# Batch 1's key maxima spread by ScalarE, and ordered behind a product of batch 0

## The chip, the cores and the metric

The kernel runs on one core of a Trainium2 chip. The metric is device time in microseconds, the median of some runs. Engines are called PE (TensorE, matmuls), DVE (VectorE), ACT (ScalarE), POOL (GpSimd) and SP (SyncE, here the queue that issues the DMAs). Each works through its own list of instructions in order; they meet through semaphores.

## What is computed

Attention over local keys and block summaries, then two feed-forward blocks. Cut to what matters here:

```python
B, H, S, D = 2, 8, 768, 64
k_sum = k.reshape(B, H, nb, 32, D).max(axis=3)       # nb = 24 blocks of 32 keys: the key maxima
v_sum = v.reshape(B, H, nb, 32, D).mean(axis=3)
scores_l = scale * q @ k.T                            # only |i - j| < 16 counts
scores_s = scale * q @ k_sum.T + log(32)              # every query sees every block
a = softmax(concat([masked scores_l, scores_s]))
x = a @ concat([v, v_sum])
x = sigmoid(xr @ w_r) * (relu(xk @ w_k) ** 2 @ w_v)   # xk, xr: mixes of x with x one row earlier
u = x + (relu(x.T @ w_tok1) @ w_tok2).T
out = u + relu(u @ w_ch1) @ w_ch2
```

## The kernel before

Attention works on six query tiles of 128 rows for each of the two batches. For a tile t the keys that its queries may see, and the 24 block maxima, stand in one tile kw: the local keys in the middle, and a copy of the maxima at either end, so that one matmul gives 120 scores. `k_max` (line 231) reduces the keys of a tile to 4 maxima with DVE, into ks. `kw_sums` (line 237) copies all 24 maxima of ks to both ends of a kw: two copies a tile, twelve a batch, and none can start before the last of the six reductions. `s_stage` multiplies queries by kw (sp, line 309), DVE reads the scores with the mask and takes the row minimum (pe and mn, line 327), ACT takes the exponential (line 329). For batch 1 `n_stage` then normalises on POOL (line 340) with a reciprocal from DVE (line 338), `t_stage` transposes (pt, line 346) and `v_stage` multiplies by the values (pv, line 366). For batch 0 the normalisation comes after that: the sums' reciprocals are spread by a matmul (rb, line 382), ACT copies pv into xT (line 385) and DVE multiplies (line 386). That is the product of x.

While attention runs, PE is filled with the first feed-forward block of the rows that are ready: `mixed` makes xk (POOL line 466, DVE line 467), its rounded upper part xh (ACT) and the rest xl (DVE, line 469); ko is xk times w_k (line 477); `k2_tile` takes relu (rl, ACT line 489), the square (DVE line 490), and splits it in kh (ACT line 491) and kl (POOL line 492); acc is that times w_v. There is one bank for ko, so the next ko waits until ACT has read the last one. The weights are 64-bit numbers that are rounded piece by piece in `Weights.step`: ACT (wst, line 148), DVE (wf, lines 152 and 158), ACT (w, line 160), POOL (its low half, line 161); there are two wf buffers, so a piece's first DVE step waits for POOL's step of the piece two before.

The program is written by hand as a mix of generators, and then a scheduler reorders each engine's list by its own estimate of durations and by priorities (`tc.high_priority`, the numbers HK, HM and so on). `behind(inst, marks)` (line 171) adds a rule for that scheduler that an instruction stands after another one. So a change at one place moves instructions at others. Batch 1 begins in `prep(1)`, which is reached while batch 0's last two tiles are still in work: key loads have come by then, and the six reductions, two value sums and the copies of the maxima are written there.

Of the kernel before, what the change touches and what calls it, by code (L numbers as in the profile page):

```python
# [14 lines left out]
ALU = mybir.AluOpType  # L15
AX = mybir.AxisListType
# [38 lines left out]
def fused_kernel(ctx, tc, q, k, v, vt, mu, w_k, w_v, w_r, w_t1, w_t2, w_c1, w_c2, out):  # L55
    nc = tc.nc
# [7 lines left out]
    NB = S // BLOCK  # L64
# [13 lines left out]
    def bank(tag, bufs, shape, name):  # L78
        return ps.tile(shape, F32, tag=tag, bufs=bufs, name=name)
# [88 lines left out]
    def in_line(inst):  # L168

        behind(inst, line[-1:])  # L170
        line.append(inst)

    def behind(inst, marks):

        for m in marks:
            tc.add_manual_dep(inst.ins, m.ins.name,
                              mybir.DependencyInfo(mybir.DependencyClass.NoSync, mybir.DependencyReason.DATA), reason="queue order")
# [23 lines left out]
    def ahead(n):  # L201

        def wrap(fn):
            def run(*args, **kw):
                with tc.high_priority(n) if n else ExitStack():
                    return fn(*args, **kw)
            return run
        return wrap
# [17 lines left out]
    def k_max(b, t):  # L226

        st = state[b]
        keys = st["kw"][t][:, :, K0 + PAD:K0 + PAD + 128].rearrange("p a (n w) -> p a n w", w=BLOCK)
        n = 128 // BLOCK  # L230
        nc.vector.tensor_reduce(st["ks"][:, :, n * t:n * t + n], keys, AX.X, ALU.max)

    @ahead(HK)
    def kw_sums(b, t):
        st = state[b]
        for o in (0, WC - NB):
            nc.gpsimd.tensor_scalar(st["kw"][t][:, :, o:o + NB], st["ks"], 1.0, 1.0, ALU.mult, ALU.mult)

    @ahead(HL)
    def vt_load(b, j):  # L240
# [112 lines left out]
    @ahead(HV)  # L353
    def v_stage(zs):
        b, t, _ = zs[0]["u"]
        st = state[b]
        if t not in st["pv"]:
            st["pv"][t] = bank("pv", 1, [128, NP, 128], "pv")
        pv = st["pv"][t]
        line.clear()  # L360
        for p in range(NP):
            for half in range(2):
                for z in zs[::-1]:
                    e = z["u"][2]
                    h = 2 * p + e
                    m = nc.tensor.matmul(pv[64 * e:64 * e + 64, p, 64 * half:64 * half + 64],  # L366
                                         st["vw"][t][half][0][:, h * D:(h + 1) * D],
                                         z["PT"][:, p, 64 * half:64 * half + 64], start=True, stop=True)
                    if len(zs) > 1:
                        in_line(m)  # L370
        if zs[-1]["u"][2] == 1:
            c0 = b * XB + 1 + 128 * t
            if b not in LATE:
                nc.scalar.copy(xT[:, :, c0:c0 + 128], pv)
            else:
                den = st["den"].pop(t)
                nc.vector.tensor_scalar(den, den, 1e-9, None, ALU.add)
                nc.vector.reciprocal(den, den)
                rb = bank("pt", 2, [128, NP, 128], "rb")
                for p in range(NP):  # L380
                    for e in range(2):
                        nc.tensor.matmul(rb[64 * e:64 * e + 64, p], den[:, e, p:p + 1].to_broadcast([128, D]), ident,
                                         start=True, stop=True)
                x = xT[:, :, c0:c0 + 128]
                nc.scalar.copy(x, pv)
                nc.vector.tensor_tensor(x, x, rb, ALU.mult)

    done_tiles = [0]

    def attention():  # L390
        slots = {}
# [2 lines left out]
        for i in range(len(steps) + 1):  # L394
            if i < len(steps):
                b, t, es = steps[i]
                if b and t == 0:
                    yield from prep(b)
                zs = s_stage(b, t, es)
                if len(es) == 1:  # L400
                    for what, z, lag in zip((t_stage, v_stage), (zs[0], zs), LAGS):
                        slots.setdefault(min(i + lag, n0), []).append(((i + lag, lag), what, z))
                else:
                    slots[i + 1] = [((i, 1), n_stage, z) for z in zs] + [((i, 2), t_stage, z) for z in zs] + [((i, 3), v_stage, zs)]
                if i < SPIN_UNITS:
                    spin(SPIN)
                yield 0.95 * len(es)
                if es[-1] == 1 and t + 1 < NT:
                    kw_sums(b, t + 1)
                if t == 0 and es[-1] == 1 - b * (len(es) == 1):  # L410
                    if b == 0:
                        v_gather(b)
                    vw_sums(b, 0)
# [34 lines left out]
    def prep(b):  # L448

        for t in range(NT):  # L450
            k_max(b, t)
            yield HOLD / (NT + 2)
        for j in range(2):
            vt_sum(b, j)
            yield HOLD / (NT + 2)
        kw_sums(b, 0)
        v_gather(b)
# [121 lines left out]
    for kind in range(3):  # L579
        mc = const.tile([128, NC], F32, name=f"mask{kind}")  # L580
        mm = work.tile([128, 2, 128], F32, tag="t32", bufs=2, name="mm")
        for half in range(2):
            m = mm[:, half, :NC]
            nc.gpsimd.memset(m, 0.0)
            first = 64 * half - PAD
            keys = m[:, NB:NC] if half == 0 else m[:, 0:NK]
# [10 lines left out]
    for t in range(NT):  # L597
        ahead(HK)(k_max)(0, t)
    kw_sums(0, 0)
    for j in range(2):  # L600
        vt_sum(0, j)
# [264 lines left out]
```

## Time and profile before

| what | value |
|---|---|
| median of 3 runs | 511.06 us (510.78 to 512.84) |
| the profiled execution | 511.19 us, span 509.4 us |
| PE busy | 492.6 us (97% of the span) |
| DVE, ACT, POOL busy | 249.1, 206.4, 186.4 us |
| granted clock of PE, mean | 0.998 |

The span runs from the first to the last instruction; the execution's own time is 1.8 us longer. Times in the views count from the start of the span. Batch 1's attention begins near 66 us and ends near 180 us; after about 255 us the second feed-forward block keeps PE busy to the end. In a timeline, a row merges neighbours of one kind, and a matmul of sp, pv or rb is recorded twice (x18 for nine).

### The profile page before, as it was taken

The page shows a single profiled execution, that of the slowest core. Times are in us where ns is not written, and L with a number is a line of the kernel's source. Part 1 is how long each engine was busy: PE and PEld are TensorE (multiplying, and loading weights), DVE is VectorE, ACT ScalarE, POOL GpSimd, SP SyncE. Part 2 cuts the span into 40 slices and gives each one's busy share as a digit, 9 for nine tenths or more (in the row PEclk, how much of TensorE's full clock was granted, in tenths as well). Part 3 has the DMA queues.
Part 4 walks back from the last instruction along what each step waited for, and adds up shares of the span by engine and source line. Part 5 has one row for each costly group of instructions (what it writes and reads, how often), then busy time and mean ns, then how long its engine had stood idle before and what let it go on. Part 6 is the DMA issues. An engine that isn't in the chain of part 4 may idle for free.

```text
span 509.4 us, 7950 instructions
## 1 busy us (share of the span) xinstructions
PE 492.6 (97%) x3064; PEld 399.6 (78%) x3064; DVE 249.1 (49%) x544; ACT 206.4 (41%) x477; POOL 186.4 (37%) x250
## 2 busy tenths in 40 slices
PE   7999897999999999999999999999999999999995
PEld 3578775788888888887888888888888888888884
DVE  3789999740515174798676576343141211311112
ACT  1689655962534444556455435343110201001000
POOL 5335567971534465697734333332100000000000
PEclk9999999999999999999999999999999999999999
DMA  8999942031000660001525650000020000200002
GB/s 254 307 295 338 333 128 71 9 100 40 21 0 14 237 248 0 1 0 42 164 85 209 235 176 1 0 1 1 0 84 0 1 0 1 82 1 0 0 1 82
DMA packets 24197, 45.40 MB, mean 89 GB/s; under 512 B 2112, under 2 KB 11328, under 8 KB 24160
## 3 DMA queue, kind: packets, MB, share of 16 engines
q1 hardware_dynamic: 24160, 44.90, 28.1%
q8 instruction: 24, 0.39, 0.3%
q14 instruction: 13, 0.11, 0.1%
HBM read 41.16 MB, written 3.15 MB: 87 GB/s over the span
## 4 chain that ended last, share of the span: by engine, by line
PE 79%; DVE 9%; POOL 4%; issue 3%; ACT 2%; DMA 2%; SPq 1%; DVEq 0%; POOLq 0%; ACTq 0%
PE o L791 19%; PE go L477 19%; PE ko L477 10%; PE acc L477 10%; PE ro L477 5%; PE ho L477 3%; PE h L477 3%; PE sp L309 3%; PE pv L366 2%; DVE xk L467 2%; PE pt L346 2%; DMA xT<-in_vt_dram 1%; PE spin L556 1%; DVE wf L152 1%; PE utr L745 1%
## 5 line engine op out<-in xcount | busy, mean ns | idle before, releaser
L477 PE MATMUL go<-u,w 128*128 128x512 f32 x432 | 106.7, 393 | 0.0
L161 POOL TENSOR_TENSOR w<-wf,w 128x512 fp32r<-128x512 f32 x50 | 68.7, 1379 | 85.5 <-ACT w L160 78.8
L477 PEld LDWEIGHTS go<-u,w 128*128 128x128 f32 x432 | 80.7, 188 | 17.5
L791 PE MATMUL o<-w,gh 128*128 128x512 f32 x288 | 89.0, 395 | 0.0
L706 DVE SCALAR_TENSOR_TENSOR gl<-go,gh 128x512 fp32r<-128x512 f32 x36 | 24.9, 691 | 121.1 <-ACT gh L705 120.9
L477 PE MATMUL ko<-xh,w 128*128 128x256 f32 x384 | 77.0, 289 | 0.7 <-ACT w L160 0.6
L705 ACT ACTIVATE gh<-go 128x512 fp32r<-128x512 f32 x36 | 21.5, 597 | 128.8 <-PE go L477 128.7
L477 PEld LDWEIGHTS ko<-xh,w 128*128 128x128 f32 x384 | 61.4, 188 | 4.5 <-issue 1.3
L791 PEld LDWEIGHTS o<-w,gh 128*128 128x128 f32 x288 | 54.0, 188 | 12.1
L477 PE MATMUL acc<-w,kh 128*128 128x512 f32 x192 | 60.7, 398 | 1.9 <-ACT kh L491 1.9
L477 PE MATMUL ko<-xl,w 128*128 128x256 f32 x192 | 54.6, 284 | 1.0 <-DVE xl L469 1.0
L791 PE MATMUL o<-w,gl 128*128 128x512 f32 x144 | 55.4, 394 | 0.0
L160 ACT CAST w<-wf 128x512 fp32r<-128x512 f32 x50 | 30.9, 619 | 47.3 <-DVE wf L158 47.1
L492 POOL TENSOR_TENSOR kl<-rl,kh 128x512 fp32r<-128x512 f32 x24 | 34.5, 1437 | 34.6 <-ACT kh L491 31.2
L466 POOL TENSOR_SCALAR tmp<-xT,oms 128x256 f32<-128x256 f32 x52 | 38.1, 742 | 23.1 <-DVE xk L467 15.0
L158 DVE SCALAR_TENSOR_TENSOR wf<-wst,wf 128x512 int32<-128x512 int32 x50 | 41.4, 834 | 8.4 <-ACT wst L148 6.9
L329 ACT ACTIVATE pe<-pe,mn 128x120 f32<-128x120 f32 x96 | 36.6, 383 | 18.5 <-DVE mn L327 18.2
L477 PEld LDWEIGHTS acc<-w,kh 128*128 128x128 f32 x192 | 34.6, 188 | 9.1 <-ACT kh L491 2.4
L490 DVE TENSOR_TENSOR rl<-rl 128x512 f32<-128x512 f32 x24 | 18.9, 785 | 46.7 <-ACT rl L489 46.3
L467 DVE SCALAR_TENSOR_TENSOR xk<-xT,mus,tmp 128x256 f32<-128x256 f32 x52 | 39.2, 784 | 4.2 <-POOL tmp L466 3.8
L477 PE MATMUL acc<-w,kl 128*128 128x512 f32 x96 | 37.1, 397 | 1.1 <-POOL kl L492 1.1
L477 PEld LDWEIGHTS ko<-xl,w 128*128 128x128 f32 x192 | 36.2, 189 | 2.1 <-DVE xl L469 1.3
(85 smaller groups left out, 695.2 us busy)
## 6 DMA issues: line engine op xcount, KB each, us to landing
wst<-in_moe_w_ch_dram SPq DMA_DIRECT2D x24, 512.0 KB, 4.6
wst<-in_moe_w_k_dram SPq DMA_DIRECT2D x8, 512.0 KB, 7.6
wst<-in_moe_w_v_dram SPq DMA_DIRECT2D x8, 512.0 KB, 10.3
kw<-in_k_dram SPq DMA_DIRECT2D x12, 320.0 KB, 8.8
wst<-in_moe_w_tok_dram SPq DMA_DIRECT2D x6, 512.0 KB, 4.5
out_dram<-o SPq DMA_DIRECT2D x12, 256.0 KB, 2.0
ybuf<-in_v_dram SPq DMA_DIRECT2D x12, 192.0 KB, 9.8
vw<-in_v_dram SPq DMA_DIRECT2D x12, 192.0 KB, 2.6
```

The lines of the kernel that those rows point to most:

```text
L158: nc.vector.scalar_tensor_tensor(wi, top, 3, wi, ALU.logical_shift_left, ALU.bitwise_or)
L160: self.rounded.append(nc.scalar.copy(hi, wf))
L161: nc.gpsimd.tensor_tensor(lo, wf, hi.bitcast(F32), ALU.subtract)
L329: nc.scalar.activation(pe, pe, AF.Exp, bias=mn[:, p:p + 1], scale=-1.0, accum_out=den[:, p:p + 1])
L466: nc.gpsimd.tensor_scalar(tmp, xT[:, d, x0 - 1:x0 - 1 + MW], om[:, d:d + 1], 1.0, ALU.mult, ALU.mult)
L467: nc.vector.scalar_tensor_tensor(xk[:, d], xT[:, d, x0:x0 + MW], mu[:, d:d + 1], tmp, ALU.mult, ALU.add)
L477: nc.tensor.matmul(o, l, r, start=(first and i == 0), stop=(last and i == 3 * n - 1))
L490: nc.vector.tensor_tensor(rl, rl, rl, ALU.mult)
L492: nc.gpsimd.tensor_tensor(lo, rl, hi.bitcast(F32), ALU.subtract)
L705: nc.scalar.activation(hi, o, AF.Relu)
L706: nc.vector.scalar_tensor_tensor(lo, o, 0.0, hi.bitcast(F32), ALU.max, ALU.subtract)
L791: nc.tensor.matmul(acc[t], l, r, start=(f == 0 and i == 0), stop=(f == nf - 1 and i == 2))
```

## The change

Batch 1's twelve copies of the key maxima are made by ACT instead of POOL; batch 0's stay on POOL. Batch 1's six reductions get a rule that they stand behind the last product of x that has been written by then (line 386 of the kernel before). When `prep(1)` is written, that is the product of key tile 4.

```diff
--- before.py
+++ after.py
@@ -228,13 +228,18 @@
         st = state[b]
         keys = st["kw"][t][:, :, K0 + PAD:K0 + PAD + 128].rearrange("p a (n w) -> p a n w", w=BLOCK)
         n = 128 // BLOCK
-        nc.vector.tensor_reduce(st["ks"][:, :, n * t:n * t + n], keys, AX.X, ALU.max)
+        m = nc.vector.tensor_reduce(st["ks"][:, :, n * t:n * t + n], keys, AX.X, ALU.max)
+        if b:
+            behind(m, ends[-1:])
 
     @ahead(HK)
     def kw_sums(b, t):
         st = state[b]
         for o in (0, WC - NB):
-            nc.gpsimd.tensor_scalar(st["kw"][t][:, :, o:o + NB], st["ks"], 1.0, 1.0, ALU.mult, ALU.mult)
+            if b:
+                nc.scalar.copy(st["kw"][t][:, :, o:o + NB], st["ks"])
+            else:
+                nc.gpsimd.tensor_scalar(st["kw"][t][:, :, o:o + NB], st["ks"], 1.0, 1.0, ALU.mult, ALU.mult)
 
     @ahead(HL)
     def vt_load(b, j):
@@ -383,9 +388,10 @@
                                          start=True, stop=True)
                 x = xT[:, :, c0:c0 + 128]
                 nc.scalar.copy(x, pv)
-                nc.vector.tensor_tensor(x, x, rb, ALU.mult)
+                ends.append(nc.vector.tensor_tensor(x, x, rb, ALU.mult))
 
     done_tiles = [0]
+    ends = []
 
     def attention():
         slots = {}
```

The scheduler's lists differ from about 56 us on (the start of the reductions) to about 170 us, and are the same in front of that and behind it. The six reductions stood on DVE between steps of xk and of weight pieces, three of them ahead of tile 4's product; they now stand behind it, three and three, with a value sum, a square and two other steps between. Three places behind that follow. Lines of the kernel after are 5 or 6 higher than those of the kernel before.

ACT, around the place where batch 1's maxima are complete. Before:

```order
L489 ACTIVATE rl<-ko 128x512
L468 CAST xh<-xk 128x1024
L160 CAST w<-wf 128x512
L148 ACTIVATE wst<-wst 128x512
L491 CAST kh<-rl 128x512
L489 ACTIVATE rl<-ko 128x512
L160 CAST w<-wf 128x512
L148 ACTIVATE wst<-wst 128x512
L491 CAST kh<-rl 128x512
L385 COPY xT<-pv 128x4x128
L160 CAST w<-wf 128x512
```

and with the change:

```order
L495 ACTIVATE rl<-ko 128x512
L474 CAST xh<-xk 128x1024
L160 CAST w<-wf 128x512
L148 ACTIVATE wst<-wst 128x512
L495 ACTIVATE rl<-ko 128x512
L497 CAST kh<-rl 128x512
L240 COPY kw<-ks 128x4x24 x12
L497 CAST kh<-rl 128x512
L160 CAST w<-wf 128x512
L148 ACTIVATE wst<-wst 128x512
L390 COPY xT<-pv 128x4x128
L160 CAST w<-wf 128x512
```

The second rl moved ahead of the first kh, the twelve copies stand behind that kh, and the next weight piece (w, wst), which stood ahead of the second kh, stands behind it.

DVE, from the last reduction (ks from kw_1108) to the first scores of batch 1 (pe_1250). Before:

```order
L231 TENSOR_REDUCE ks_447<-kw_1108 128x4x4
L152 TENSOR_SCALAR wf_932<-wst_153 128x512
L158 SCALAR_TENSOR_TENSOR wf_832<-wst_151,wf_832 128x512
L351 COPY PT_1319<-pt_1314 120x512
L490 TENSOR_TENSOR rl_757<-rl_757 128x512
L253 TENSOR_REDUCE vrs_1205<-ybuf_71 128x48
L158 SCALAR_TENSOR_TENSOR wf_932<-wst_153,wf_932 128x512
L152 TENSOR_SCALAR wf_955<-wst_155 128x512
L158 SCALAR_TENSOR_TENSOR wf_955<-wst_155,wf_955 128x512
L386 TENSOR_TENSOR xT_84<-xT_84,rb_1350 128x4x128
L327 ISA pe_1250,mn_1248<-sp_1230,mask1_183 128x120
```

and with the change:

```order
L231 TENSOR_REDUCE ks_447<-kw_1108 128x4x4
L152 TENSOR_SCALAR wf_932<-wst_153 128x512
L356 COPY PT_1319<-pt_1314 120x512
L496 TENSOR_TENSOR rl_757<-rl_757 128x512
L158 SCALAR_TENSOR_TENSOR wf_832<-wst_151,wf_832 128x512
L258 TENSOR_REDUCE vrs_1205<-ybuf_71 128x48
L158 SCALAR_TENSOR_TENSOR wf_932<-wst_153,wf_932 128x512
L391 TENSOR_TENSOR xT_84<-xT_84,rb_1350 128x4x128
L152 TENSOR_SCALAR wf_955<-wst_155 128x512
L332 ISA pe_1250,mn_1248<-sp_1230,mask1_183 128x120
```

The product of tile 5 (xT, with rb_1350) moved ahead of the weight piece wf_955; that piece's second step now comes after four of the eight score reads.

PE, at the scores of batch 1's second tile. Before:

```order
L309 MATMUL sp<-kw,qT 64x120 x10
L477 MATMUL ko<-xh,w 128x256
L477 MATMUL ko<-xl,w 128x256
L477 MATMUL ko<-xh,w 128x256 x2
L477 MATMUL ko<-xl,w 128x256
L477 MATMUL ko<-xh,w 128x256 x2
L477 MATMUL ko<-xl,w 128x256
L477 MATMUL ko<-xh,w 128x256 x2
L477 MATMUL ko<-xl,w 128x256
L477 MATMUL ko<-xh,w 128x256
L309 MATMUL sp<-kw,qT 64x120 x6
L477 MATMUL acc<-w,kh 128x512 x4
```

and with the change:

```order
L314 MATMUL sp<-kw,qT 64x120 x16
L351 MATMUL pt<-ident,pe 120x128
L483 MATMUL ko<-xh,w 128x256
L483 MATMUL ko<-xl,w 128x256
L483 MATMUL ko<-xh,w 128x256 x2
L483 MATMUL ko<-xl,w 128x256
L483 MATMUL ko<-xh,w 128x256 x2
L483 MATMUL ko<-xl,w 128x256
L483 MATMUL ko<-xh,w 128x256 x2
L483 MATMUL ko<-xl,w 128x256
L483 MATMUL ko<-xh,w 128x256
L351 MATMUL pt<-ident,pe 120x128 x3
```

The sixteen scores stand together, and the first transpose of batch 1 (pt) stands ahead of twelve products of ko; acc, which came before the transposes, comes later.

## Rows read from the trace of the kernel before

**Rows 1.** Busy time by stretches: us, then engines, granted clock, DMA, GB/s.

```profile
core 0: us, PE busy (x) PEld busy (x) DVE busy (x) ACT busy (x) POOL busy (x), PEclk, DMA share, GB/s
...
66.00:97.00 31.00, 26.86 (x240) 20.31 (x239) 27.86 (x81) 18.79 (x57) 25.34 (x40) 1.00 0.24 66
97.00:205.00 108.00, 108.00 (x882) 92.90 (x881) 43.61 (x112) 52.78 (x132) 55.72 (x74) 1.00 0.24 78
205.00:240.00 35.00, 33.88 (x193) 29.34 (x192) 30.66 (x39) 20.59 (x34) 26.25 (x24) 1.00 0.03 7
```

**Rows 2.** Timeline of PE: start, duration, instruction, [idle before, releaser].

```profile
82.22 0.82 PE L309 MATMUL sp<-kw,qT 64*64 64x120 f32 x18 [0.38 <-DVE mn L327]
...
90.92 0.65 PE L346 MATMUL pt<-ident,pe 128*120 128x128 f32 x4
...
95.27 1.00 PE L346 MATMUL pt<-ident,pe 128*120 128x128 f32 x3 [0.28 <-POOL pe L340]
```

**Rows 3.** Waits of PE, 66 to 97 us.

```profile
engine line waited for: us in total, times, longest us
PE acc L477 <- ACT kh L491: 1.9, 2, 1.0
PE sp L309 <- issue: 0.9, 1, 0.9
PE ko L477 <- ACT w L160: 0.6, 1, 0.6
```

**Rows 4.** Timeline of DVE, 67 to 80 us.

```profile
67.11 1.26 DVE L231 TENSOR_REDUCE ks<-kw 128x16 f32<-128x512 f32 x2
68.30 1.65 DVE L469 TENSOR_TENSOR xl<-xk,xh 128x1024 fp32r<-128x1024 f32 x1
69.88 0.67 DVE L231 TENSOR_REDUCE ks<-kw 128x16 f32<-128x512 f32 x1
70.47 0.41 DVE L152 TENSOR_SCALAR wf<-wst 128x512 int32<-128x512 int32 x1
70.81 0.74 DVE L158 SCALAR_TENSOR_TENSOR wf<-wst,wf 128x512 int32<-128x512 int32 x1
71.47 0.68 DVE L351 COPY PT<-pt 120x512 f32<-120x512 f32 x1
72.07 0.67 DVE L490 TENSOR_TENSOR rl<-rl 128x512 f32<-128x512 f32 x1
72.67 1.74 DVE L253 TENSOR_REDUCE vrs<-ybuf 128x48 f32<-128x1536 f32 x1
74.34 0.72 DVE L158 SCALAR_TENSOR_TENSOR wf<-wst,wf 128x512 int32<-128x512 int32 x1
76.24 1.48 DVE L152 TENSOR_SCALAR wf<-wst 128x512 int32<-128x512 int32 x1 [1.19 <-POOL w L161]
77.82 1.60 DVE L158 SCALAR_TENSOR_TENSOR wf<-wst,wf 128x512 int32<-128x512 int32 x1
79.34 0.67 DVE L386 TENSOR_TENSOR xT<-xT,rb 128x512 f32<-128x512 f32 x1
```

**Rows 5.** Timeline of POOL, 66 to 89 us.

```profile
67.58 1.29 POOL L492 TENSOR_TENSOR kl<-rl,kh 128x512 fp32r<-128x512 f32 x1 [1.27 <-ACT kh L491]
70.64 3.88 POOL L237 TENSOR_SCALAR kw<-ks 128x96 f32<-128x96 f32 x12 [1.77 <-DVE ks L231]
...
88.99 0.58 POOL L340 TENSOR_SCALAR pe<-pe,den 128x120 f32<-128x120 f32 x1 [0.54 <-DVE den L338]
```

**Rows 6.** Groups of ACT: count, busy us, mean ns, idle before.

```profile
L160 ACT CAST w<-wf 128x512 fp32r<-128x512 f32 x50 | 30.9, 619 | 47.3 <-DVE wf L158 47.1
...
L468 ACT CAST xh<-xk 128x1024 fp32r<-128x1024 f32 x13 | 13.6, 1044 | 6.2 <-DVE xk L467 5.6 <-PE ro L477 0.5
```

**Rows 7.** Timeline of ACT at 71 us.

```profile
71.64 0.62 ACT L160 CAST w<-wf 128x512 fp32r<-128x512 f32 x1 [3.64 <-DVE wf L158]
72.17 0.70 ACT L148 ACTIVATE wst<-wst 128x512 f32<-128x512 f32 x1
```

**Rows 8.** Chain that ended last, at 96 us: start, us, what.

```profile
96.27 2.25 PE ko L477 x19
```

**Rows 9.** Stretches at the end, columns as in rows 1.

```profile
503.00:504.00 1.00, 0.54 (x3) 0.11 (x1) 1.00 (x2) 0.00 (x0) 0.00 (x0) 1.00 0.00 0
...
508.00:509.00 1.00, 0.00 (x0) 0.00 (x0) 0.00 (x0) 0.00 (x0) 0.00 (x0) 0.50 0.03 8
```

## The prediction

> **What bounds the kernel now.** I read the busy time of each engine by stretches first. The stretch from 97 to 205 us has TensorE (PE) busy for 108.00 of 108.00 us, and from 205 to 240 us for 33.88 of 35.00 [rows 1]. PE is the bound there, and whatever the other engines do in those stretches is hidden. In the stretch from 66 to 97 us, where batch 1's attention starts, PE is busy for 26.86 of 31.00 us: 4.14 us of idle time [rows 1]. The change works in this stretch alone, and PE's matmuls are the same before and after, so 4.1 us is nearly all that it can win. I say nearly, because some waiting hides in rows that count as busy: three transposes took 1.00 us at 95.27 where four took 0.65 at 90.92 [rows 2], so some 0.5 us more.
>
> The list of what PE waited for comes second [rows 3]: 1.9 us for kh on ScalarE (ACT) in two waits, 0.9 us before the scores sp with no releaser that the trace names ("issue"), 0.6 us for a weight piece that ACT rounds; then 0.38 us for the score reads of VectorE (DVE) at 82.22 and 0.28 us for the normalised exponentials of GpSimd (POOL) at 95.27 [rows 2]. None of these waits names the copies of the key maxima. They are late steps of queues in which the maxima and their copies stand. So the change is worth what it does to those queues, and that needs a walk through the new order.
>
> **The change part by part.** The six reductions of batch 1 (kw into ks) are held behind the product of x that was the last one that the program has written by then. That is the product of key tile 4, not of tile 5, since tile 5's is written later. DVE does the same set of steps before the last reduction as now, only in another order, so I keep the end of the last reduction at 69.88 + 0.67 = 70.55 [rows 4]. Cost 0; what could move it is one step more or less that is held by POOL, of the size of xl's 1.65 at 68.30, which ended 1.1 us after POOL's kl (67.58 + 1.29 = 68.87) [rows 4, 5]. I take half a microsecond either way.
>
> The twelve copies leave POOL, where they took 3.88 us [rows 5], and go to ACT. The trace has no copy of 96 elements on ACT. A cast of 1024 elements takes 1.044 us and one of 512 takes 0.619 [rows 6]: 0.83 ns an element, 0.19 fixed, so 0.27 us for 96 elements. Neighbours overlap: a row of 0.62 us at 71.64 is followed by the next at 72.17, 0.53 later [rows 7], so 0.18 from start to start, 2.2 us for twelve. The ends are 3.3 us (no overlap) and 2.0; I take 2.2, since ACT's rows in a line all overlap. The copies run from 70.6 to 72.9.
>
> **ACT, POOL and DVE behind the copies.** On ACT the second rl is now issued ahead of the first kh, and PE does twelve products for ko before it needs that kh. So PE starts at 66.7 and not 67.56: the 0.84 us at 67.56, one of the two waits for kh, goes. From 72.9 ACT does the second kh (about when it did before), then at 73.5 the weight cast that it did at 71.64 [rows 7], then the copy of x at 74.6. POOL, free of the copies, does its kl from 73.5 to 74.8 (1.29, [rows 5]) and the weight's low half to 76.1. DVE from 70.55, with the gaps between starts of [rows 4]: mask work 0.34, PT 0.60, rl 0.60, shift 0.66, vrs 1.67, which is 74.4; the next shift waits for POOL's kl and ends at 75.4. Then comes the product of tile 5, at 75.4 and not at 79.34: the two steps of the following weight piece, which waited 1.19 us and took 1.48 and 1.60 [rows 4], stand behind it now. From that product to the release of PE at 82.22 DVE took 2.9 us; with one weight step more, its second one held by POOL, it is about 4.0. Scores are released at 79.4. PE had done all that stands before them at about 80.6 (82.22 less the waits of 0.38 and 0.9 and a matmul of 0.4); by the 0.84 that it won it is there at 79.7. So the waits of 0.9 and 0.38 go as well.
>
> **What is late next.** PE now does all sixteen scores of the next tile (nine, recorded as x18, took 0.82 us at 82.22 [rows 2], so some 1.2) to 80.9, and then its order has a transpose of the first exponential ahead of the twelve ko products. That transpose needs POOL's normalisation, which needs DVE's reciprocal, and that stands on DVE behind three steps of xk, two of a weight piece and a small one: 3.3 us after 79.4, with the second weight step held by one POOL piece of 1.3. So POOL starts at 82.75 (before: 88.99 [rows 5]), PE goes on at 83.1 and has **a new wait of 2.2 us**. The twelve ko products (1.4 us at 2.25/19 each [rows 8]) then run together with the rest, and the next scores wait for DVE's reads, which stand behind the square of rl, which POOL holds for 1.3 us: **a new wait of 1.0 us**. The old waits of 1.05 for kh, 0.62 for the weight cast and 0.28 are passed by work that was ordered ahead of them.
>
> The sum: 4.1 us of idle time goes, 0.5 hidden goes, 2.2 + 1.0 = 3.2 comes: 1.4 us less. After 97 us PE has no idle time to take more [rows 1], and its matmuls are the same, so the shift is carried to the end. The profiled execution took 511.19 us, 0.13 above the median of 511.06; 1.4 less gives 509.8 for the execution, 509.7 for the median. A difference of 0.5% (2.55 us) is about what a measurement of this kernel can tell from none. **I forecast 509.7, within 0.5%**, with 508.6 to 510.7 as its own range (each hand-off in the walk may be 0.1 us off, and there are ten in a row).
>
> **Rivals.** *More is won.* If DVE's chain to the reciprocal is a microsecond or two shorter (xk and the shift not held by POOL), the new wait at the transpose all but disappears and 2.6 to 4.1 us is won: 508.5 to 507.0. For it: the same steps take 0.66 to 0.74 when POOL is not in their way [rows 4]. Against it: of the DVE steps at 76.24 and 77.82, both were held to more than twice that [rows 4]. 0.20.
>
> *POOL's copies hold DVE.* If the 3.88 us of copies kept DVE out, DVE would be freed of up to that and all behind it would come 3.9 us sooner: 507.2. Rows speak against it: the shift at 70.81 took 0.74 us and the square at 72.07 took 0.67, both while the copies ran from 70.64 on [rows 4, 5], against 0.72 for the shift at 74.34. The Trainium skill, SBUF — State Buffer, Who interferes with whom, says that GpSimd and a VectorE step with two SBUF inputs lock each other out, whole instructions at a time; by it this rival would win. The trace agrees for POOL's big subtractions and does not show it for these copies. 0.03.
>
> *Nothing is left.* The new waits reach 4.6 us, or the 1.4 us are lost at the next place where PE waits, the 1.1 us of idle time between 205 and 240 us [rows 1]: 510.6 to 512. For it: the walk adds no delay for a hand-off. Against: PE is never idle in the 108 us between. 0.13.
>
> *Slower: PE is tied to POOL's normalisation.* PE takes its instructions in order, and the transpose now stands in front of twelve ko products that need nothing from it. In the present trace the normalisation began at 88.99 [rows 5]; if the longer ACT queue (copies, kh, two weight casts, then the exponentials) keeps it there, PE goes on at 89.1 instead of 83.1, 6.0 us later, and the sum is +4.6: 515.7. It decides from a reciprocal 1.4 us later than my 82.7, and is past 0.5% from 4.0 later, at 86.7. Against it: all that it hangs on starts 2 to 4 us sooner in the walk. So long a stop could also touch PE's clock: it was granted in full while PE worked up to 504 us and half of it (1.2 GHz) after PE had stood still, at 508 to 509 [rows 9]; at half the clock the twelve ko products would cost 1.4 us more. The Trainium skill, TensorE: Matmul & The Clock Gate, What's actually happening, says that an idle array falls to half its rate; the trace agrees at its end, and the waits of rows 3 left the clock at 1.00. 0.14.
>
> **How the numbers follow.** Forecast 0.50, more won 0.20, lock 0.03, nothing 0.13, slower 0.14. Faster by over 0.5%: the second and third, and a tail of the first, 0.25. Slower by over 0.5%: 0.15. Within: 0.60. The range takes the first and fourth whole, most of the second (from 507.4) and the start of the last: 507.4 to 513.0.
>
> **What would show it.** Right: copies of some 0.27 us on ACT between 70 and 74 us; the product of tile 5 near 75.5; one PE wait of 2 to 2.5 us for POOL's pe near 81 to 83; no PE idle time from 97 to 205. Wrong: PE's idle time in 66 to 97 below 2 us or above 6; copies of 0.4 us or more; the reciprocal later than 85; a granted clock below 1.00; or new idle time of PE after 97 us.

## The result: 515.32 us, slower by 0.6%, and the profile after

| | before | after |
|---|---|---|
| median of 9 runs each | 511.52 us (510.78 to 516.93) | 515.32 us (513.12 to 520.17) |
| ratio | | 1.0059, 95% interval 1.0038 to 1.0081 |
| profiled execution, its span | 511.19 us, 509.4 us | 515.32 us, 513.4 us |
| PE busy | 492.6 us | 496.1 us |
| granted clock of PE, mean | 0.998 | 0.988 |

The ratio is that of the measurement, with its interval; the quotient of the two medians alone is 1.0074. The forecast was 509.7 and no change; the time lies outside the range. The span grew by 4.0 us. PE has the same matmuls to do, yet it is busy for 3.5 us longer, and idle for only 0.5 us longer. So the first thing to look for is matmuls that took longer, not a wait. The page of the changed kernel shows where, in its row of the granted clock (40 slices of 12.8 us):

```profile
span 513.4 us, 7945 instructions
...
PE 496.1 (97%) x3064; PEld 403.6 (79%) x3064; DVE 247.7 (48%) x544; ACT 209.1 (41%) x489; POOL 182.6 (36%) x238
...
PEclk9999997899999999999999999999999999999999
```

The seventh and eighth slice are below full: 77 to 103 us, the place where batch 1's attention starts. The busy time by stretches of the changed kernel (columns as in [rows 1]), first the stretches of [rows 1], then three of 5 us:

```profile
66.00:97.00 31.00, 26.41 (x229) 21.56 (x228) 27.69 (x86) 22.37 (x77) 21.86 (x28) 0.83 0.20 54
97.00:205.00 108.00, 108.00 (x875) 92.49 (x874) 42.35 (x108) 49.54 (x119) 53.49 (x72) 1.00 0.24 78
205.00:240.00 35.00, 33.83 (x188) 29.03 (x187) 27.43 (x35) 21.34 (x34) 26.09 (x23) 1.00 0.00 1
80.00:85.00 5.00, 2.37 (x41) 1.78 (x39) 5.00 (x17) 4.36 (x17) 3.76 (x4) 0.92 0.23 52
85.00:90.00 5.00, 4.34 (x19) 3.70 (x19) 5.00 (x24) 3.80 (x15) 4.77 (x6) 0.50 0.46 147
90.00:95.00 5.00, 5.00 (x46) 4.47 (x47) 3.12 (x18) 4.17 (x18) 5.00 (x11) 0.55 0.00 0
```

PE's idle time from 66 to 97 us was 4.14 us and is 4.59: nothing of it went away. From 97 to 205 us there is none, as before, and from 205 to 240 us it is 1.17 us where it was 1.12. New is the granted clock: 0.92, 0.50 and 0.55 where it was 1.00 throughout. The record of the clock gives the edges: half (1.2 GHz of 2.4) from 84.24 to 94.48 us, 10.24 us long. Before, PE fell to half only at 507.4 us, after its last matmul. What PE waited for from 66 to 97 us, in the changed kernel (columns as in [rows 3]):

```profile
PE pt L351 <- POOL pe L345: 3.3, 1, 3.3
PE vp L265 <- DVE vrs L258: 1.1, 1, 1.1
PE sp L314 <- ACT kw L240: 0.2, 1, 0.2
```

The six waits of [rows 2, 3], none longer than 1.05 us, have become one of 3.3 us, one of 1.1 and a short one. PE's timeline of the changed kernel around the long one (columns as in [rows 2]):

```profile
80.92 1.45 PE L314 MATMUL sp<-kw,qT 64*64 64x120 f32 x32
85.66 0.47 PE L351 MATMUL pt<-ident,pe 128*120 128x128 f32 x1 [3.30 <-POOL pe L345]
85.78 0.56 PE L483 MATMUL ko<-xh,w 128*128 128x256 f32 x1
...
88.28 0.41 PE L483 MATMUL ko<-xh,w 128*128 128x256 f32 x1
...
90.58 1.87 PE L314 MATMUL sp<-kw,qT 64*64 64x120 f32 x30
```

The sixteen scores end at 82.37 us, PE stands still until POOL's normalised exponential comes at 85.66, and in the middle of this wait, 1.9 us after the last matmul, the clock falls. The twelve ko products then take from 85.78 to 88.49: 2.71 us, where 12 of them were priced at 1.4 from [rows 8].

Why the wait ends so late is read on the other engines. DVE of the changed kernel (columns as in [rows 4]):

```profile
63.14 0.68 DVE L391 TENSOR_TENSOR xT<-xT,rb 128x512 f32<-128x512 f32 x1
63.74 1.86 DVE L231 TENSOR_REDUCE ks<-kw 128x16 f32<-128x512 f32 x3
65.52 1.74 DVE L258 TENSOR_REDUCE vrs<-ybuf 128x48 f32<-128x1536 f32 x1
...
68.11 0.67 DVE L231 TENSOR_REDUCE ks<-kw 128x16 f32<-128x512 f32 x1
68.71 2.24 DVE L475 TENSOR_TENSOR xl<-xk,xh 128x1024 fp32r<-128x1024 f32 x1
70.88 1.27 DVE L231 TENSOR_REDUCE ks<-kw 128x16 f32<-128x512 f32 x2
...
76.71 0.67 DVE L391 TENSOR_TENSOR xT<-xT,rb 128x512 f32<-128x512 f32 x1
...
79.11 1.34 DVE L158 SCALAR_TENSOR_TENSOR wf<-wst,wf 128x512 int32<-128x512 int32 x1
...
82.54 1.22 DVE L342 TENSOR_SCALAR den<-den 128x4 f32<-128x4 f32 x1
...
84.90 0.17 DVE L343 RECIPROCAL den<-den 128x4 f32<-128x4 f32 x1
```

POOL's timeline of the same execution (columns as in [rows 5]):

```profile
68.59 1.29 POOL L498 TENSOR_TENSOR kl<-rl,kh 128x512 fp32r<-128x512 f32 x1 [3.00 <-ACT kh L497]
...
78.62 1.29 POOL L161 TENSOR_TENSOR w<-wf,w 128x512 fp32r<-128x512 f32 x1
...
82.32 1.43 POOL L161 TENSOR_TENSOR w<-wf,w 128x512 fp32r<-128x512 f32 x1
...
85.23 2.09 POOL L345 TENSOR_SCALAR pe<-pe,den 128x120 f32<-128x120 f32 x4 [0.52 <-DVE den L343]
```

And the copies on ACT, in ACT's timeline (columns as in [rows 7]):

```profile
72.18 2.17 ACT L240 COPY kw<-ks 128x96 f32<-128x96 f32 x12 [3.67 <-DVE ks L231]
```

Three reductions now stand directly behind tile 4's product (63.14) and directly ahead of the value sum vrs, which ends at 67.26; PE's vp waits for it for 1.14 us (1.1 in the list of waits). That wait has come in the place of the 0.84 us for kh at 67.56. Of the other three reductions one stands ahead of the big step xl and two behind it; before, it was two ahead and one behind [rows 4]. xl is held by POOL's kl, as in [rows 4, 5], only longer (2.24 us for 1.65), since kl now comes a microsecond later: in both kernels xl ends 1.1 us after kl does. So the maxima are complete at 72.15, not at 70.55. Two more DVE steps run long beside a low half on POOL on the way to the reciprocal: 1.34 us at 79.11, where POOL's ends at 79.91, and 1.22 us for a step on four numbers at 82.54, which ends with POOL's at 83.75. The reciprocal comes at 84.90.

### The profile page after: what moved, and what is told of

Read it like the earlier page. It is cut to its first block, busy times and chain, and to the rows that moved or that the text cites. A ratio compares the mean times of both kernels' runs of the same rounds, so it can differ in the third digit from the quotient of the medians.

```text
span 513.4 us, 7945 instructions
## 1 busy us (share of the span) xinstructions
PE 496.1 (97%) x3064; PEld 403.6 (79%) x3064; DVE 247.7 (48%) x544; ACT 209.1 (41%) x489; POOL 182.6 (36%) x238
## 4 chain that ended last, share of the span: by engine, by line
PE 76%; DMA 10%; DVE 5%; SPq 2%; POOL 2%; issue 2%; ACT 1%; DVEq 0%; POOLq 0%; ACTq 0%
PE o L797 19%; PE go L483 19%; PE ko L483 11%; PE acc L483 10%; PE ro L483 5%; PE ho L483 3%; PE h L483 3%; DMA ybuf<-in_v_dram 2%; DMA wst<-in_moe_w_k_dram 2%; DMA xT<-in_vt_dram 2%; PE sp L314 2%; SPq L224 2%; DMA xT<-in_q_dram 2%; DMA wst<-in_moe_w_v_dram 1%; DMA vw<-in_v_dram 1%
## 5 line engine op out<-in xcount | busy, mean ns | idle before, releaser
L161 POOL TENSOR_TENSOR w<-wf,w 128x512 fp32r<-128x512 f32 x50 | 69.2, 1388 | 84.1 <-ACT w L160 82.7
L483 PE MATMUL ko<-xh,w 128*128 128x256 f32 x384 | 79.3, 295 | 0.1
L483 PEld LDWEIGHTS ko<-xh,w 128*128 128x128 f32 x384 | 63.3, 194 | 3.8 <-issue 1.6
L483 PE MATMUL ko<-xl,w 128*128 128x256 f32 x192 | 56.0, 292 | 1.0 <-DVE xl L475 1.0
L158 DVE SCALAR_TENSOR_TENSOR wf<-wst,wf 128x512 int32<-128x512 int32 x50 | 40.2, 811 | 8.1 <-ACT wst L148 6.7
```

The lines of the kernel that those rows point to most:

```text
L158: nc.vector.scalar_tensor_tensor(wi, top, 3, wi, ALU.logical_shift_left, ALU.bitwise_or)
L161: nc.gpsimd.tensor_tensor(lo, wf, hi.bitcast(F32), ALU.subtract)
L483: nc.tensor.matmul(o, l, r, start=(first and i == 0), stop=(last and i == 3 * n - 1))
```

## The experiments

Three theories stood at the start. *Clock*: the loss is PE's work at half the clock behind one long wait; with the wait broken up it would be gone. *Waits and order*: the new order of the queues makes PE late, whatever the clock. *Copies*: ACT's longer queue delays what PE needs. In the table, the **net shift** is the growth of the span against the profiled execution of before, less the delay that was there already at the first ko product of attention (51.32 us before, 51.56 in the changed kernel), since what stands in front of it varies from execution to execution. The half-clock stretch is the one that lies in batch 1's attention.

| kernel | median us, ratio [95%] | PE's wait at the first pt | half clock, us | net shift, us |
|---|---|---|---|---|
| changed | 515.32, 1.0059 [1.0038, 1.0081] | 3.30 | 84.24 to 94.48 | +3.8 |
| changed, again | 514.90, 1.0050 [1.0032, 1.0068] | 3.30 | 85.27 to 88.68 | +1.8 |
| one idle matmul | 512.36, 1.0007 [0.9993, 1.0021] | 2.25 | 85.12 to 88.53 | +0.6 |
| two idle matmuls | 512.37, 1.0010 [0.9988, 1.0032] | 1.39 | none | +0.9 |
| four idle matmuls | 515.24, 1.0052 [1.0032, 1.0072] | none | 92.96 to 96.37 | +2.4 |
| transpose later | 514.82, 1.0044 [1.0017, 1.0070] | 0.70 (and 1.50 before ko) | 89.88 to 96.70 | +3.8 |
| transpose later, two idle | 514.22, 1.0046 [1.0026, 1.0065] | 0.70 | 89.65 to 96.47 | +3.2 |
| copies on ACT alone | 513.83, 1.0028 [1.0007, 1.0050] | 1.26 (and 1.09 before ko) | 87.09 to 93.91 | +2.0 |
| same, two idle | 513.04, 1.0026 [1.0012, 1.0041] | 1.19 | none | +1.4 |
| rule alone | 514.47, 1.0039 [1.0015, 1.0063] | 3.11 | 85.14 to 95.38 | +3.5 |
| same, two idle | 513.39, 1.0036 [1.0019, 1.0053] | 1.35 | none | +1.4 |
| before, one idle | 511.89, 1.0011 [0.9996, 1.0026] | none | none | +0.6 |

**Two idle matmuls in the wait.** PE multiplies the identity by itself into the transposes' bank, which the transposes then overwrite. It adds work to PE and takes none away. It is not the only thing that differs, though: with it the scheduler also writes other lists behind the wait, here for all four engines.

```diff
+        if z["u"] == (1, 0, 0):
+            for _ in range(2):
+                behind(nc.tensor.matmul(pt, ident, ident.unsqueeze(1).to_broadcast([128, 4, 128]), start=True, stop=True), mark[-2:])
```

> The changed kernel with two idle matmuls of 128x512 on PE (0.43 us each) ahead of that first transpose, so that the wait for POOL stays and PE is busy in part of it. Clock theory: PE goes on at the same point (85 to 86 us), the granted clock stays at 1.00, 511.5 to 513. Chain theory: 515 or above, whatever the clock.

PE's timeline of the kernel with two idle matmuls (the row at 81.89 holds them, recorded as x4; they take about 1 us each, not 0.43):

```profile
81.89 1.98 PE L352 MATMUL pt<-ident 128*128 128x512 f32 x4
85.27 0.33 PE L354 MATMUL pt<-ident,pe 128*120 128x128 f32 x1 [1.39 <-POOL pe L345]
...
89.37 0.84 PE L314 MATMUL sp<-kw,qT 64*64 64x120 f32 x22 [1.24 <-DVE mn L332]
```

PE goes on at 85.27, 0.39 us sooner than in the changed kernel; its first ko product came 0.39 sooner as well, at 51.17, so this is an earlier start of the whole program. The wait's end has not moved; the time behind it has. The clock stayed full, and the time is 512.37. Seven of the twelve runs had a mean clock of 0.997 or more and took 511.9 to 512.4; the five at 0.994 or 0.995 took 513.4 to 514.1. The wait of 1.24 us for the next score reads now shows; it is the second new wait of the prediction.

**One idle matmul, and the changed kernel once more on the same chip.** The same edit with `range(1)`; and the changed kernel as it is.

> The changed kernel with one idle matmul (128 by 512, about 1 us) ahead of batch 1's first transpose; DVE's list is the changed kernel's to the letter. The wait for POOL's pe shrinks from 3.3 to about 2.3 us and PE goes on at about 85.7 as before. Clock theory (the loss is PE's time at half clock behind the long wait): where the clock stays at 1.00 the run is at 512 to 512.8; where it still falls, at 514.5 to 515.7; so the runs split by their mean clock (0.997 and 0.988), and nothing lies at 515 with a clock of 0.997. Rival (the kernel with two idle matmuls was quick because its DVE order differs): this one, with the order unchanged, stays at 515 whatever its clock says.

> The changed kernel once more, as it is, beside the two with idle matmuls on one chip. 513.1 to 515.6 with a median of about 515 and a clock of 0.988 to 0.994; half the clock from about 84 to 94 us in the profiled execution. If it came at 512.5 or below with the same order, the loss would be the chip's or the run's and not the change's.

One idle matmul took the median from 514.90 to 512.36. Its runs went from 511.3 to 513.7, and none was near 515. DVE's list is that of the changed kernel, so another DVE order is not what makes it quick. But the lists of PE, ACT and POOL differ from the changed kernel's behind the wait, and the rival that another order of those is the cause stands. The split that I expected did not come: in the profiled execution the clock did fall, for 3.41 us, and the time was 511.33 all the same. PE's timeline of the kernel with one idle matmul:

```profile
81.45 1.13 PE L352 MATMUL pt<-ident 128*128 128x512 f32 x2
84.82 0.32 PE L354 MATMUL pt<-ident,pe 128*120 128x128 f32 x1 [2.25 <-POOL pe L345]
...
89.13 1.05 PE L314 MATMUL sp<-kw,qT 64*64 64x120 f32 x30
...
104.56 1.15 PE L374 MATMUL pv<-PT,vw 120*64 120x64 f32 x32
```

and one stretch of the same execution (columns as in [rows 1]):

```profile
85.00:90.00 5.00, 5.00 (x50) 4.26 (x49) 5.00 (x24) 4.22 (x17) 5.00 (x7) 0.66 0.38 132
```

The changed kernel once more, PE's timeline:

```profile
85.29 0.47 PE L351 MATMUL pt<-ident,pe 128*120 128x128 f32 x1 [3.30 <-POOL pe L345]
...
89.61 1.04 PE L314 MATMUL sp<-kw,qT 64*64 64x120 f32 x30
...
106.16 1.15 PE L371 MATMUL pv<-PT,vw 120*64 120x64 f32 x32
```

and two stretches:

```profile
85.00:90.00 5.00, 4.71 (x36) 4.14 (x40) 5.00 (x23) 3.87 (x15) 5.00 (x7) 0.66 0.45 147
90.00:95.00 5.00, 4.85 (x52) 3.90 (x44) 4.16 (x25) 5.00 (x21) 5.00 (x11) 1.00 0.00 0
```

This execution and the changed kernel's first say most. With the same lists and the same wait of 3.30 us, the clock is back at 1.00 from 90 us on where it was 0.55: this execution was at half clock for 3.41 us and the first for 10.24 (I had expected the long stretch again), and the net shift is 1.8 us here and 3.8 there. Less the difference in their start, the two are level on PE up to 88.9 us, where the clock returns in one of them; they are 2.4 us apart near 94 and 2.0 from 95 on. So **2.0 us of the first one's loss is the clock alone**. The runs show both levels: here four at a mean clock of 0.994 took 513.0 to 513.4 us, five at 0.988 to 0.991 took 514.8 to 515.5, and three at 0.985 or less took 516.6 to 521.1; in the first measurement three at 0.994 took 513.1 to 513.5, five at 0.988 to 0.991 took 515.1 to 515.6, and one at 0.978 took 520.2.

The other comparison is this execution with that of one idle matmul. Both were at half clock for 3.41 us, and PE reaches the next scores 0.48 us apart (89.13 and 89.61), which is the difference of their starts (50.72 and 51.20 at the first ko product). At the pv of 104.56 and 106.16 they are 1.60 us apart: 1.1 us more, lost at full clock, where the lists differ, and within rounding that is the difference of the net shifts (0.6 and 1.8). So **part of what the idle matmul wins, 1.1 of 2.5 us if these two executions stand for their kernels, is the order that came with it, and not the clock**.

**Four idle matmuls.** `range(4)`, 3.7 us of work, more than the wait.

> Four idle matmuls, about 4 us, more than the wait of 3.3. Clock theory: no wait at the transpose, PE goes on some 0.5 to 0.8 us later than in the changed kernel, clock at 1.00, 512.4 to 513.2: slower than two idle matmuls by what PE goes on later, quicker than the changed kernel by 2 us or more although PE has more to do. Rival (order, not clock): 515 or above, since PE has more work and the maxima, the reciprocal and the normalisation come no sooner.

That was missed: 515.24. The wait at the transposes is gone, but PE is now held up further on, from 89.9 to 91.78, by POOL's low half of a weight piece (x2, two pieces, of which the second ends near 91.7), and the clock falls at 92.96, 1.2 us after that wait. PE's timeline of this kernel (the row at 83.77 holds the idle matmuls):

```profile
83.77 3.70 PE L352 MATMUL pt<-ident 128*128 128x512 f32 x8
...
91.78 0.51 PE L486 MATMUL ko<-xh,w 128*128 128x256 f32 x2 [1.87 <-POOL w L161]
```

and POOL's:

```profile
86.71 2.10 POOL L345 TENSOR_SCALAR pe<-pe,den 128x120 f32<-128x120 f32 x4 [0.52 <-DVE den L343]
88.77 2.96 POOL L161 TENSOR_TENSOR w<-wf,w 128x512 fp32r<-128x512 f32 x2
```

The six runs lie between 513.4 and 515.6, the two at a mean clock of 0.996 and more at 513.4 and 513.9. Filling the whole wait was no cure in this order: the next release that PE needs is POOL's. With 3.41 us at half clock, as with one idle matmul, the net shift is 2.4 us and not 0.6, so the length of that stretch does not tell the two apart.

**The transpose later.** The first transpose of batch 1 is held behind ko's products, so that PE has the twelve to do in the wait; only PE's list differs from the changed kernel's.

```diff
-            nc.tensor.transpose(pt[:NC, p], z["P"][p], ident)
+            tr = nc.tensor.transpose(pt[:NC, p], z["P"][p], ident)
+            if z["u"] == (1, 0, 0):
+                behind(tr, [kos[0, 3, 0]])
```

> The changed kernel, with one thing moved: on PE, the first transpose of batch 1 stands behind the twelve ko products instead of ahead of them; every other list is the same. Clock theory (the wait of 3.3 us ahead of that transpose let PE's clock fall to half, and some 9 us of work at half the clock is most of the loss): PE's longest wait in the stretch is about 1.5 us (until ScalarE has read the ko bank), granted clock 1.00 to the end, 511.5 to 513. Chain theory (the clock is a side effect; DVE and POOL set the pace there): the wait is shorter but comes back at the next scores, clock 1.00 or not, 514.5 to 515.5.

PE's waits of this kernel, 66 to 97 us:

```profile
PE ko L488 <- ACT rl L502: 1.5, 1, 1.5
PE sp L315 <- DVE mn L333: 1.3, 1, 1.3
...
PE pt L352 <- POOL pe L346: 0.7, 1, 0.7
```

and one stretch:

```profile
90.00:95.00 5.00, 4.22 (x41) 3.92 (x42) 3.75 (x24) 4.72 (x20) 5.00 (x10) 0.50 0.00 0
```

The one wait became 1.50, 0.70 and 1.28 us: PE had worked ahead and met the bank of ko, which waits for ACT. The sum is no smaller, and the clock fell at 89.88 all the same, at the last of the three. The net shift is 3.8 us as in the first execution of the changed kernel, with a half-clock stretch of 6.82 us for its 10.24. The 514.82 us and the wait at the next scores are what the chain theory forecast. So the place of the transpose alone does not carry the loss, and a wait of over 3 us is not needed for it. With two idle matmuls added to this kernel:

> The changed kernel with the first transpose behind the twelve ko products, and two idle matmuls where PE then waits for ScalarE (1.5 us). Clock theory: the same total of waits as before, a full clock, 511.5 to 512.5. Chain theory: 514 to 515, as without the idle matmuls.

PE's timeline of that kernel:

```profile
87.80 1.01 PE L355 MATMUL pt<-ident,pe 128*120 128x128 f32 x3 [0.70 <-POOL pe L346]
...
90.88 1.47 PE L315 MATMUL sp<-kw,qT 64*64 64x120 f32 x22 [1.29 <-DVE mn L333]
```

The clock theory's forecast was missed: the wait for ko went, the waits of 0.70 and 1.29 us stayed, and the clock fell at 89.65, where the second of them had just begun. The 514.22 us is what the chain theory said.

**Each half of the change by itself.** The rule without the move to ACT, and the move without the rule, each also with the two idle matmuls:

```diff
 rule alone
-            if b:
+            if False:
                 nc.scalar.copy(st["kw"][t][:, :, o:o + NB], st["ks"])
 copies on ACT alone
-            behind(m, ends[-1:])
+            behind(m, [])
```

> The other half: the reductions behind the product of x, copies on GpSimd as before. Its list on PE has two transposes ahead of the twelve ko products. Clock theory: a wait of 3 us or more ahead of them, the clock falls, 514 to 516. If ScalarE's longer list is the cost of the change: 510 to 512.

> Half of the change: batch 1's copies on ScalarE, without the rule that the reductions stand behind the product of x. Clock theory: what counts is whether PE waits over 3 us ahead of batch 1's first transpose; its list has ten ko products ahead of that transpose here, so no such wait, clock 1.00, 510 to 512. If ScalarE's longer list is the cost: a loss like that of the whole change, 514 to 516.

> The rule alone (copies on GpSimd), with two idle matmuls on PE ahead of batch 1's first transpose. Clock theory: what made that kernel slower (514.5) was the clock that fell in the 3 us of waiting; with PE busy in part of it the clock stays at 1.00 in most executions and the time is 511.5 to 512.6. If the order of the work itself is slow (chain theory): 514 or more at a full clock.

> The copies on ScalarE alone, with two idle matmuls on PE ahead of batch 1's first transpose. Clock theory: 511.5 to 512.8 at a clock of 0.997 or more, against 513.8 without them. Chain theory: 513.5 or more, at a full clock.

The rule alone gives nearly the whole picture: a wait of 3.11 us at the same transpose, the same 10.24 us at half clock, 514.47 us, although its copies are still POOL's. POOL's timeline of that kernel:

```profile
71.89 3.88 POOL L242 TENSOR_SCALAR kw<-ks 128x96 f32<-128x96 f32 x12 [2.37 <-DVE ks L231]
```

and PE's:

```profile
85.84 0.47 PE L351 MATMUL pt<-ident,pe 128*120 128x128 f32 x1 [3.11 <-POOL pe L345]
```

So the copies on ACT are not needed for the loss. They are not free either: alone they cost too (513.83), with waits of 0.86, 1.09 and 1.26 us and 6.82 us at half clock; the expectation that the clock would stay full was missed, though no wait is over 1.3 us. Whether that is ACT's longer queue or the order that the scheduler then writes was not tried. The net shifts of the halves, 3.5 and 2.0 us, do not add up to the 3.8 of the whole. With two idle matmuls both halves kept a full clock in the profiled execution, and both were still 1.4 us late; both medians (513.39 and 513.04) lie between what the two theories forecast. The last reduction in DVE's timeline of the copies-alone kernel:

```profile
71.67 0.67 DVE L231 TENSOR_REDUCE ks<-kw 128x16 f32<-128x512 f32 x1
```

Its program came 1.79 us later from the start on, so it stands at 69.88, exactly where it was in [rows 4]. In the kernel of the rule alone the maxima were complete at 71.79, and in the changed one at 72.15: with the start of each program taken off (0.10 us sooner, 0.24 later), 1.3 to 1.4 us later than before. So it is the rule that makes the maxima late. And PE's vp waits 1.1 to 1.2 us in each of the nine profiled executions here that have the rule, and in none of the four without.

**An idle matmul in the kernel before.** The edit of two idle matmuls, with `range(1)`, in the kernel before.

> The kernel before with one idle matmul on PE where it waits 1.05 us for kh (at 85 us). Clock theory: the kernel before keeps its clock through these waits in nearly all executions, so nothing is won: 511.0 to 512.2, ratio 0.999 to 1.001. If part of its own executions lose the clock there (those of 513 us): those become rarer and the median falls by up to 0.5 us.

511.89 beside 511.85: nothing is to be won there with idle work; the clock was full in that stretch anyway. Its profiled execution had a half-clock stretch of another kind, of which the last section tells.

## Why the prediction was wrong

Where it was right, by its steps:
- The copies on ACT run 0.17 us apart: twelve in 2.17 us, for 2.2 forecast.
- The long wait stands where it was put, at the first transpose, for POOL's pe. The score wait of 0.38 and the 0.9 ahead of it are gone, and so are the waits for kh.
- The product of tile 5 moved forward, to 76.71 (forecast 75.4, before 79.34).
- The second new wait is there in the kernel with two idle matmuls, whose clock was full: 1.24 us, for 1.0 forecast. In the changed kernel it does not show. A reason, argued only: PE at half speed comes later than the reads.
- No idle time from 97 to 205 us, and what was lost by 170 us is carried to the end. Of its signs of being wrong, only the granted clock came.

Where it failed:
- **"I keep the end of the last reduction at 70.55 ... half a microsecond either way."** It came at 72.15. DVE does the same steps before it, as the prediction says, but the order was given a cost of 0: the rule bunches three reductions ahead of vrs and puts one more of the others behind xl, which meets POOL's kl. That the rule does it is shown by the two halves, above.
- **"A new wait of 2.2 us."** It is 3.30. The late maxima (1.6), and two steps that run long beside POOL's, put the reciprocal at 84.90 for 82.7; PE came to the place at 82.37 for 80.9.
- The walk looked at the waits that the change removes and at those at its end, and not at vrs, which the three reductions now stand in front of: 1.14 us at vp.
- **The sum took a microsecond of waiting as a microsecond, and had no term for the clock.** What showed in its place is 10.24 us at half clock, of which 6.83 cost 2.0 us. The side remark in the slower rival, that twelve ko products would cost 1.4 us more at half the clock, was right in size (2.71 for 1.4), but it was tied to a stop of 6 us and had no term of its own. Half the clock came with a stop of 3.3.

The account: the forecast was −1.4, the span grew by 4.0, a difference of 5.4. Idle time from 66 to 97 us is 4.59 for the 3.2 of the walk: 1.4 (1.1 at pt, 1.14 at vp, 0.15 for the copies at sp, less the 1.0 that did not show). The other 4.0 is PE's busy time: 0.5 less was forecast, and it is 3.5 longer. Of these, 1.6 is the longer half-clock stretch: with the same lists PE was busy for 494.4 us in the second execution of the changed kernel, and for 496.1 in the first. The remaining 1.9 is there with 3.41 us at half clock too. By the ko products, which took 2.71 us for 1.4, that stretch would cost 1.6 (an estimate), but no execution of these lists at a full clock shows it, and other lists, those with one idle matmul, ended 1.1 us sooner with as long a stretch. The time of the slower rival, 515.7, was met closely by luck, in another way: the normalisation came 3.8 us sooner than before (85.23 for 88.99), and a reciprocal at 84.90, 2.2 late, would by that rival's rule have left the time within 0.5%. The kernel with two idle matmuls does stay within: a ratio of 1.0010 at a kept clock, the case in which nothing is left, though in another order.

Why is nothing left, even then? The rows suggest that the stretch is paced by DVE, busy for 27.69 us of the 31 (27.86 before), and by POOL's subtractions that hold it; taking 3.88 us from POOL leaves DVE's work as it is. That reading was not tried by itself. What is shown is that PE's waiting did not go: its waits of over 0.1 us between 55 and 170 us add up to 4.45 us before, 4.86 with the change, 5.93 with the rule alone and 3.75 with the copies on ACT alone.

What stays open: how the 1.8 us that the changed kernel loses with the shorter stretch divide between the clock and the order; how the 0.6 to 1.4 us of the kernels with idle matmuls divide between those matmuls and the order; and why the same wait of 3.30 us led to a half-clock stretch of 3.4 us in one execution and 10.2 in another. No kernel here was faster than the one before.

## What to carry to other kernels

Price a stop of the busiest engine by two terms, its length and what the work behind it costs if the clock falls. The clock fell here with one wait of 3.30 us, but also with waits of 0.70 and 1.29, so short waits are no assurance. To price the clock, compare executions of the same lists that differ in the clock; an edit that keeps the clock up, as the idle matmul, moves other instructions too, and its gain is then not the clock's alone. When an instruction of an in-order queue that needs a long chain is moved ahead of ready work, walk that chain in the new order, with every step that another engine may hold. A rule given to a scheduler for one step moves what stands around it: look for what it bunches, and for who waits behind the bunch.

## What was not expected of the hardware

- A wait of 3.30 us on PE was followed by half the clock for 3.41 us in one execution and 10.24 us in another of the same program. The fall came 1.9 us into the wait in one of them, and in the other at the very end of it (85.27, with PE going on at 85.29).
- The clock fell without a long wait too: in the kernel with the later transpose and two idle matmuls it fell at 89.65 us, 0.06 us into a wait of 1.29 and 1.85 after one of 0.70, with no other wait of over 0.2 us since 69 us. In the kernel with two idle matmuls alone it stayed full over waits of 1.39 and 1.24.
- The cost is below what the stretch suggests. 6.83 us more at half clock, in two executions of the same lists, cost 2.0 us. The Trainium skill, TensorE: Matmul & The Clock Gate, HAM oscillation — how this bites in real kernels, reckons the extra time at half of the throttled time, which would be 3.4 us here, an estimate; the runs show less. A part of the reason is in the rows: of the longer stretch, 1.42 us (84.24 to 85.66) lay in the wait, where PE had nothing to do. Near 94 us the two executions were 2.4 us apart, and some 0.4 us of that came back just behind, where the quicker one waits for POOL's kl (0.15 us at 94.50).
- Five of the thirteen profiled executions have an early fall as well. In that of the kernel before with one idle matmul it lay from 17.96 to 21.38 us, where PE is busy. A stretch of it:

```profile
18.00:21.00 3.00, 3.00 (x8) 1.41 (x8) 2.70 (x19) 1.97 (x11) 0.08 (x1) 0.50 1.12 304
```

The first score product of this execution came 0.03 us later than in the kernel before, its first ko product 1.65 us later, and the rest of the program carried that on. In the five executions with such a fall the first ko product came at 52.58 to 53.11 us, in the other eight at 50.72 to 51.56. So single times of one kernel can differ by some 1.5 us for it, and the table compares net shifts.
